# The last chunk of a three-product mixture layer, computed by Strassen on its two token halves

## The chip, the core and the metric

The kernel runs as one program on one core of a Trainium2 chip. The metric is the device time of one execution in microseconds (us). The kernel before took 1428.8, 1425.85 and 1426.25 us in three timed runs, median 1426.25.

## The reference

Three layers run one after the other: a linear attention with a norm, a dense gated mixture over 4608 tokens (512 wide, 1536 hidden), and a mixture of 8 experts of which each token takes one.

```python
x = attn_out.transpose(0, 2, 1, 3).reshape(4608, 512)
xn = x / sqrt(mean(x * x, -1) + 1e-6) * rms_g      # the first mixture
g, val = xn @ w_gate, xn @ w_val                   # 512 -> 1536
x = (silu(g) * val) @ w_out                        # 1536 -> 512
logits = x @ w_gate2                               # the second: 8 experts
e = argmax(logits)
out = prob[e] * (relu(x @ w1[e]) @ w2[e])          # 512 -> 1024 -> 512
```

The change is in `xn @ w_gate` and `xn @ w_val` for the last 512 tokens.

## The kernel before

**Tiling.** The 4608 tokens are 9 chunks of 512. Each fp32 product is three matmuls on split operands, high by high, low by high and high by low (`mm3`, L148); a `split` (L143) makes the high half on ScalarE (ACT) and the low half on VectorE (DVE). The hidden width is 12 tiles `f` of 128, each with a gate and a value half, so 24 `product`s a chunk. Chunks 0 to 3 take them plainly, 12 matmuls of 512 columns each. Chunks 4 to 7 go in two pairs by Strassen: seven products in the order 5, 1, 2, 6, 7, 3, 4 with weight sums that chunk 0 to 3 leave in DRAM (`wst`); class `Ring` (L1173) streams those on ACT's DMA queue into 3 slots of its own and 2 extra ones.

**Chunk 8 before** (L1958) is plain: for each `f` a gate product into the bank `pg`, SiLU on ACT (L1964), a value product into `pv`, and a multiplication on DVE (L1973). Class `Stream` (L1236) reads its weights back from `wst` on SyncE's (SP's) queue as tiles `lg` and `lv`, 512 KB each. The last `period` of chunks 6 and 7 (L1746) splits the chunk's inputs (`tstep`, L819 on ACT and L820 on DVE).

**What runs between the products.** After every product the code places pieces of other work by hand: `outs.drain(n)` gives n groups `po` of the down projection (an `mm3` of 512 columns; four groups take one 512 KB load of `wo` on SP's queue, L943, three buffers), `outs.stage` and `outs.low` split the hidden `h` into `ahl` (ACT L1651, DVE L1659), and `group()` (L1577) gives router logits of the chunk before (`junk`, DVE L992) and one step of the queue `rq`: `choose`, `exp`, `rank` and, after chunk 7, `order_step` and `start_expert`. `begin_route` (L1570) starts a chunk's route when its `po` groups are done and empties what is left of the route before.

**Towards the experts.** `rank` gives 28 small matmuls `rk` and ten small DVE operations, the last of which updates `acc`. `order_step` (L1335) counts tokens by a matmul `cnt` on `acc` and sorts the experts by load on DVE (L1346 to L1356) into `ordi`. SP reads `ordi` and loads expert weights `re` by it (L185), and `feed.step` (L292) splits them: `we` on ACT (L145), then its low half on DVE (L146). Each engine takes its instructions in the order in which they were issued.

Of the kernel before, what the change touches and what calls it, by code (L numbers as in the profile page):

```python
# [22 lines left out]
P = 128  # L23
# [22 lines left out]
AHL = 2  # L46
STAGED = 3
MORE = 2
LEFT = 7
SUPER = ((4, 5), (6, 7))  # L50
SINGLE = SUPER[0][0]
# [17 lines left out]
def attention_moe_kernel(  # L69
# [529 lines left out]
    def mark(kind, fn):  # L599
        kinds[fn] = kind  # L600
        return fn
# [571 lines left out]
    class Ring:  # L1173


        def __init__(self):
            ids = [(n, j) for _ in SUPER for n in range(2 * NPAIR) for j in range(7)]
            self.todo = deque(zip(ids[0::2], ids[1::2]))
            self.loaded, self.free, self.extra, self.done = deque(), RING, 0, []

        def fill(self, extra=MORE):
            while self.todo and (self.free or self.extra < extra):
                (n0, j0), (n1, j1) = self.todo[0]
                if n0 not in made or n1 not in made:
                    break
                own = self.free > 0
                if own:
                    self.free -= 1
                    w = rslot(f"r{n0}_{j0}")
                elif live[0] <= NSLOT - 3:  # L1190
                    self.extra += 1
                    w = wslot(f"r{n0}_{j0}")
                else:
                    break
                self.todo.popleft()
                d = w.bitcast(F32)
                if n0 == n1:
                    nc.scalar.dma_start(
                        d.rearrange("p (h n) -> p h n", h=2), blocks_of(n0, j0, j1)
                    )  # L1200
# [32 lines left out]
        if last and pn not in cur.apart:  # L1233
            live[0] -= 2

    class Stream:  # L1236


        def __init__(self):
            self.todo = deque((f, kind) for f in range(NF1) for kind in "gv")  # L1240
            self.free, self.held = RING, deque()

        def fill(self, tags=True):
            while self.todo and (self.free * tags or len(self.held) < 8 and live[0] <= NSLOT - 8):
                f, kind = self.todo.popleft()
                own = tags and self.free > 0
                w = (rslot if own else wslot)(f"l{kind}{f}")
                self.free -= own
                self.held.append(own)
                d, n = w.bitcast(F32), 2 * (f // 2) + (kind == "v")  # L1250
                if f % 2 == 0:
                    nc.sync.dma_start(d.rearrange("p (h n) -> p h n", h=2), blocks_of(n, 1, 2))
                else:
                    nc.sync.dma_start(d[:, 0:512], blocks_of(n, LEFT))
                    nc.sync.dma_start(d[:, 512:1024], blocks_of(n, 5))
                (wg if kind == "g" else wv)[f] = w

        def used(self):
            self.fill()
            own = self.held.popleft()  # L1260
            self.free += own
            live[0] -= not own

    class NextX:

# [284 lines left out]
    def start_feed():  # L1550
        feeds.append(feed)

    def flush_route():
        while logit_q:
            route.logit(*logit_q.popleft())
            if not logit_q:
                after_logits()
        while rq:
            rq.popleft()()

    def after_logits():
        r = route
        rq.extend([mark("v", r.choose), idle, idle, mark("t", r.exp), idle, mark("v", r.rank)])
        if r.c == 7:
            rq.extend([idle, idle, order_step])
            rq.extend(lambda i=i: start_expert(i) for i in range(3))
            rq.append(start_feed)
            rq.extend(lambda i=i: start_expert(i) for i in range(3, E))

    def begin_route(c, po):  # L1570
# [46 lines left out]
    gated, pace = set(), [0, 0]  # L1617

    class Out:

# [125 lines left out]
    def period(s, p, cur, nx):  # L1746
# [31 lines left out]
        def after(k):  # L1778
            if last and k == 0:
                while aux:  # L1780
                    aux.popleft()()
            barred = last and k == 4
            outs.drain(plan[k], s)
            outs.low()
            outs.stage()
            if not outs.ready and not outs.cur:
                outs.low()
            if p == 0 and cur.left:
                cur.more()
            elif nx and p > 7 and k in (0, 1, 4, 6) and not aux:  # L1790
                nx.more(2 if last else 5)
            elif last and k in (0, 1, 2, 4):
                tstep(8, (0, 1, 2, 0, 3)[k])
            elif last:
                stream.fill(False)
# [36 lines left out]
        after(6)  # L1832

    hs = []
    stream = Stream()

    for c in range(SINGLE):
        end = c == SINGLE - 1
# [117 lines left out]
    stream.fill()  # L1956
    for f in range(NF1):
        pg = psg.tile([P, 512], F32, tag="g", name=f"pg{c}_{f}")  # L1958
        if f % 2 == 0:
            h8 = hslot(f"h8_{f}")  # L1960
        h = h8[0][:, f % 2]
        product(pg, f, "g")
        stream.used()
        nc.scalar.activation(h, pg, AF.Silu)  # L1964
        for n in (3, 3) if f < 4 else (2, 1):
            outs.drain(n)
            outs.low()
            outs.stage()
            group(2 + (f < 4))
        pv = psg.tile([P, 512], F32, tag="v", name=f"pv{c}_{f}")  # L1970
        product(pv, f, "v")
        stream.used()
        nc.vector.tensor_tensor(h, h, pv, op=ALU.mult)  # L1973
        outs.add(c, h, h8[1])
        for n in (4, 3, 3) if f < 4 else (1, 0, 0):
            outs.drain(n)
            outs.low()
            outs.stage()
            group(2)
    live[0] -= KD  # L1980
    turned = False
    while outs.sets:
        if outs.sets[0]["left"] == 1 and not outs.cur and not turned:
# [244 lines left out]
```

## Time and profile before

| | |
|---|---|
| timed runs, median | 1426.25 us (1425.85 to 1428.8) |
| profiled execution, its own time | 1428.12 us |
| its span | 1426.2 us |
| TensorE (PE) busy in the span | 1404.1 us, 98% |
| VectorE busy | 918.2 us, 64% |
| ScalarE busy | 596.1 us, 42% |
| mean granted TensorE clock | 0.996 |
| chunk 8, from its first product to the first expert's transposes | 826.70 to 967.25 us |

The page gives busy time for each engine; matmuls are pipelined, so a matmul's duration is longer than the distance from its start to the next one's, and costs below are taken from starts. A bracket at the end of a timeline row is the engine's idle time ahead of it and what ended that.

### The profile page before, as it was taken

The page shows a single profiled execution, that of the slowest core. Times are in us where ns is not written, and L with a number is a line of the kernel's source. Part 1 is how long each engine was busy: PE and PEld are TensorE (multiplying, and loading weights), DVE is VectorE, ACT ScalarE, POOL GpSimd, SP SyncE. Part 2 cuts the span into 40 slices and gives each one's busy share as a digit, 9 for nine tenths or more (in the row PEclk, how much of TensorE's full clock was granted, in tenths as well). Part 3 has the DMA queues.
Part 4 walks back from the last instruction along what each step waited for, and adds up shares of the span by engine and source line. Part 5 has one row for each costly group of instructions (what it writes and reads, how often), then busy time and mean ns, then how long its engine had stood idle before and what let it go on. Part 6 is the DMA issues. An engine that isn't in the chain of part 4 may idle for free. (4 is left out here: it accounts for less than half of the span.)

```text
span 1426.2 us, 21177 instructions
## 1 busy us (share of the span) xinstructions
PE 1404.1 (98%) x7708; PEld 1182.4 (83%) x7708; DVE 918.2 (64%) x1931; ACT 596.1 (42%) x1112; POOL 200.1 (14%) x207
## 2 busy tenths in 40 slices
PE   7999999999999999999999999999999999999998
PEld 6777888878888878887888887889999989988986
DVE  5887775786778465565666356853553688578672
ACT  5775323333435433443232322243333556656651
POOL 2110101100220201001000100022404202302111
PEclk9999999999999999999999999999999999999999
DMA  7977735755763766567566575772423334334320
GB/s 239 304 231 253 249 116 175 261 184 190 235 218 111 264 231 212 175 208 257 197 204 195 163 265 193 221 237 75 144 75 122 104 109 144 121 106 141 121 82 35
DMA packets 112970, 255.52 MB, mean 179 GB/s; under 512 B 13803, under 2 KB 26347, under 8 KB 112864
## 3 DMA queue, kind: packets, MB, share of 16 engines
q1 hardware_dynamic: 81376, 190.24, 40.6%
q10 hardware_dynamic: 23040, 44.05, 9.7%
q0 software_dynamic: 8448, 19.85, 4.3%
q8 instruction: 62, 1.02, 0.3%
q14 instruction: 44, 0.36, 0.1%
HBM read 199.69 MB, written 55.28 MB: 179 GB/s over the span
## 5 line engine op out<-in xcount | busy, mean ns | idle before, releaser
L992 DVE SCALAR_TENSOR_TENSOR junk<-x,wgb 128x512 bf16<-128x512 f32 x256 | 189.4, 740 | 5.1 <-ACT x L968 0.2
L149 PE MATMUL po<-wo,ahl 128*128 128x512 f32 x408 | 160.6, 394 | 0.9 <-DVE x L970 0.9
L150 PE MATMUL po<-wo,ahl 128*128 128x512 f32 x408 | 159.0, 390 | 0.0
L151 PE MATMUL po<-wo,ahl 128*128 128x512 f32 x408 | 158.9, 390 | 0.0
L1227 PE MATMUL A<-xp,r 128*128 128x512 f32 x504 | 130.0, 393 | 1.0 <-DVE X L1812 0.8
L1065 POOL DMA_INDIRECT idxd<-rec,si x36 | 38.7, 1075 | 548.7 <-DVE cs L1074 447.1
L1227 PEld LDWEIGHTS A<-xp,r 128*128 128x128 f32 x504 | 93.3, 188 | 21.6 <-DVE X L1812 1.7
L1227 PE MATMUL X<-xp,r 128*128 128x512 f32 x360 | 93.4, 395 | 2.8 <-DMA r<-wst 1.2
L709 POOL TENSOR_TENSOR sg<-sq,smalls 128x512 f32<-128x512 f32 x36 | 49.5, 1377 | 319.5 <-ACT sq L691 242.1
L149 PEld LDWEIGHTS po<-wo,ahl 128*128 128x128 f32 x408 | 76.7, 188 | 17.1 <-DVE x L970 1.4
L151 PEld LDWEIGHTS po<-wo,ahl 128*128 128x128 f32 x408 | 76.6, 188 | 16.3
L150 PEld LDWEIGHTS po<-wo,ahl 128*128 128x128 f32 x408 | 76.6, 188 | 15.5
L1227 PEld LDWEIGHTS X<-xp,r 128*128 128x128 f32 x360 | 66.3, 188 | 18.4 <-ACT X L1803 2.0
L149 PE MATMUL pg<-x,wg 128*128 128x512 f32 x192 | 77.2, 402 | 0.1
L149 PE MATMUL pv<-x,wv 128*128 128x512 f32 x192 | 76.1, 397 | 0.6 <-DVE sl L1873 0.6
L151 PE MATMUL pg<-x,wg 128*128 128x512 f32 x192 | 75.1, 391 | 0.6 <-DVE x L820 0.6
L150 PE MATMUL pg<-x,wg 128*128 128x512 f32 x192 | 74.9, 390 | 0.6 <-DVE wg L928 0.6
L150 PE MATMUL pv<-x,wv 128*128 128x512 f32 x192 | 75.0, 391 | 0.0
L151 PE MATMUL pv<-x,wv 128*128 128x512 f32 x192 | 74.9, 390 | 0.0
L1874 ACT ACTIVATE ahl<-sl 128x512 fp32r<-128x512 f32 x42 | 26.5, 632 | 111.3 <-DVE sl L1873 111.3
L235 ACT ACTIVATE wo<-re 128x512 fp32r<-128x512 f32 x84 | 51.1, 626 | 31.8 <-DVE re L246 31.2
L1856 ACT ACTIVATE sl<-pg 128x512 f32<-128x512 f32 x48 | 28.7, 598 | 83.2 <-PE pg L151 68.1
(803 smaller groups left out, 3322.5 us busy)
## 6 DMA issues: line engine op xcount, KB each, us to landing
wo<-wos SPq DMA_DIRECT2D x90, 512.0 KB
r<-wst ACTq DMA_DIRECT2D x72, 512.0 KB
re<-in_moe_w SPq DMA_DIRECT2D x64, 512.0 KB
x1d<-x SPq DMA_DIRECT2D x32, 256.0 KB
k<-in_k SPq DMA_DIRECT2D x30, 256.0 KB
v<-in_v SPq DMA_DIRECT2D x30, 256.0 KB
q<-in_q SPq DMA_DIRECT2D x30, 256.0 KB
rg<-in_moe_w_gate SPq DMA_DIRECT2D x12, 512.0 KB
```

Source lines behind the costliest of these rows:

```text
L149: nc.tensor.matmul(ps, lhi, rhi, start=first, stop=False)
L150: nc.tensor.matmul(ps, llo, rhi, start=False, stop=False)
L151: nc.tensor.matmul(ps, lhi, rlo, start=False, stop=last)
L235: nc.scalar.activation(w[:, 0], part(n), AF.Copy)
L709: nc.gpsimd.tensor_tensor(sg, sq3, g2b[:, None, :].to_broadcast([P, 8, HD]), op=ALU.mult)
L992: nc.vector.scalar_tensor_tensor(j, self.rows[t], 1.0, wgb[e], op0=ALU.mult, op1=ALU.mult, accum_out=self.L[:, t, e : e + 1],)
L1065: nc.gpsimd.indirect_dma_start(out=idxd[:], out_offset=bass.IndirectOffsetOnAxis(ap=si[:, j : j + 1], axis=0), in_=rec[:, j, :], in_offset ...
L1227: nc.tensor.matmul(ps, w[:, a, kk, :], x[kk][b], start=first and kk == j == 0, stop=kk == 1 and j == 2, skip_group_check=True,)
L1856: nc.scalar.activation(sl, pg, AF.Silu)
L1874: nc.scalar.activation(ahl[:, 0:512], sl, AF.Copy)
```

## The change

Chunk 8's 24 plain products become 6 pairs of `f` by 7 Strassen products by gate and value: 84 products of six matmuls of 256 columns (L2020 of the new kernel). The two halves that Strassen needs are the chunk's two sets of 256 tokens, two halves of the contraction, and two neighbouring `f`. Each pair has accumulators `X` and `A` for the gate half, and `X..v` and `A..v` for the value half, the last two in banks of the pool that `rk` and `cnt` use too. Their results are put together between the products: copies on ACT after products 5 and 1 (L2036, L2038), additions on DVE after 6 and 7 (L2042, L2044), SiLU on ACT (L2031) and multiplications on DVE (L2033) for the four quarters of `h`. Because these banks are taken, `rank` and `order_step` are held (`hold`, `banked`) until a pair's last product is in; what is held of chunk 6's and 7's routes runs at the end of pairs 1 and 3.

`LastX` takes the place of the input splits: it turns the inputs, makes four sums, and splits seven operands, in the last period and in pair 0. `Stream` is gone; `Ring` has 42 more entries, each of two 256 KB loads, on SP's queue, with up to 6 extra slots. `PLAN` spreads 98 `po` groups over the pairs, 14 places in each. `feed.step` keeps more free slots while the ring has work.

```diff
+EXTRA = 6
+PLAN = (44,20,8,8,9,9)
...
             self.todo = deque(zip(ids[0::2], ids[1::2]))
+            self.todo.extend(
+                ((2 * i, j), (2 * i + 1, j)) for i in range(NPAIR) for j in range(7)
+            )
...
+                eng = nc.sync if len(self.todo) <= 7 * NPAIR else nc.scalar
...
-                    nc.scalar.dma_start(d[:, 0:512], blocks_of(n0, j0))
-                    nc.scalar.dma_start(d[:, 512:1024], blocks_of(n1, j1))
+                    eng.dma_start(d[:, 0:512], blocks_of(n0, j0))
+                    eng.dma_start(d[:, 512:1024], blocks_of(n1, j1))
...
-    class Stream:
+    class LastX:
...
+            if pn == "sum":
+                u = wslot("xu").bitcast(F32).rearrange("p (s k n) -> p s k n", s=2, k=2)
+                self.u = [u[:, i] for i in range(2)]
+                tt(self.u[0], b[0], b[1], op=ALU.add)
+                tt(self.u[1], self.u[0], a[0], op=ALU.subtract)
+                tt(b[0], b[0], a[0], op=ALU.subtract)
+                return
...
+            split(w[:, 0], w[:, 1], src)
...
+        banked.update((r.rank, order_step))
...
-        flush_route()
-        route = Route(c, po)
-        route.store()
+        flush_logits()
+        new = Route(c, po)
+        new.store()
+        if not hold[0]:
+            flush_route()
+        route = new
...
+            if hold[0] and fn in banked:
+                return True
...
-            feed.step(spare=2)
+            feed.step(spare=2 + (EXTRA - ring.extra) * bool(ring.todo))
...
-        product(pg, f, "g")
...
+    def between(k, g, i):
+        at, n = 2 * k + g, PLAN[i]
+        hold[0] = at < 13
+
+        def free(last):
+            while at == 13 and rq and (rq[0] is idle or rq[0] in banked):
+                if rq[0] is order_step and not last:
+                    break
+                rq.popleft()()
+
+        free(False)
+        ring.fill(EXTRA)
+        outs.drain((at + 1) * n // 14 - at * n // 14)
+        outs.low()
+        outs.stage()
+        lastx.more()
+        free(True)
+        group(2 if i < 2 else 1)
+
+    for i in range(NPAIR):
+        X = [psg.tile([P, 512], F32, tag="v", name=f"X8_{i}"), ptile(f"X8_{i}v")]
+        A = [psg.tile([P, 512], F32, tag="g", name=f"A8_{i}"), ptile(f"A8_{i}v")]
...
+        for k, pn in enumerate(ORDER):
+            for g in range(2):
...
+                        nc.tensor.matmul(
+                            ps, w[:, wq, kk, :], lastx.ops[pn][:, xq, kk],
+                            start=k < 2 and kk == j == 0, stop=kk == 1 and j == 2,
...
+                if pn == 5:
+                    nc.scalar.copy(s_, x)
+                elif pn == 1:
+                    nc.scalar.copy(x, a)
+                elif pn == 2:
+                    put(0, 0, x)
+                elif pn == 6:
+                    nc.vector.tensor_tensor(x, a, s_, op=ALU.add)
+                elif pn == 7:
+                    nc.vector.tensor_tensor(s_, a, s_, op=ALU.add)
+                    put(1, 1, s_)
...
+                between(k, g, i)
```

**Place 1, TensorE around the count of tokens.** `X` and `A` are accumulators, `xp` an operand of the inputs, `r` weight sums. Before:

```order
L149 MATMUL po_3_7950<-wo,ahl_8109 128x512
L150 MATMUL po_3_7950<-wo,ahl_8109 128x512
L151 MATMUL po_3_7950<-wo,ahl_8109 128x512
L1338 LDWEIGHTS ones
L1338 MATMUL cnt<-acc,ones 128x8
L149 MATMUL po_0_7947<-wo,ahl_8180 128x512
L150 MATMUL po_0_7947<-wo,ahl_8180 128x512
L151 MATMUL po_0_7947<-wo,ahl_8180 128x512
L149 MATMUL pv_8_8390<-x_0_7297,lv_8067 128x512
```

After:

```order
L151 MATMUL po_0_8024<-wo,ahl_8307 128x512
...
L1358 LDWEIGHTS ones
L1358 MATMUL cnt<-acc,ones 128x8
L2020 MATMUL X_4_8616<-xp_5_7365,r_0_8284 128x256 x6
L2020 MATMUL X_4v<-xp_5_7365,r_0_8284 128x256 x6
...
L2020 MATMUL A_4_8618<-xp_1_7387,r_1_8324 128x256 x6
L2020 MATMUL A_4v<-xp_1_7387,r_1_8324 128x256 x6
...
L2020 MATMUL X_4_8616<-xp_2_7390,r_2_8349 128x256 x6
L151 MATMUL po_3_8027<-wo,ahl_8307 128x512
...
L2020 MATMUL X_4v<-xp_2_7390,r_2_8349 128x256 x6
```

The count stood behind a gate product and two `po` groups after `rk`; now one `po` group is between. Behind it there were a `po` group and a 512-column product; now the products of pair 4, the third of which (product 2, `xp_2`) adds to what a copy on ACT leaves in `X_4` and `X_4v`. Each `po` group is three matmuls, of which one or two are shown; one more stands after `X_4v<-xp_5` and one after `A_4v<-xp_1`.

**Place 2, ScalarE where the first expert's weights are split.** `re_0`, `re_1` are raw expert weights. Before:

```order
L1964 ACT_TABLE_LOAD
L1964 ACTIVATE h_8_8295<-pg_8_8294 128x512
L1651 ACTIVATE ahl_8407<-h_8_8295 128x512
L145 ACTIVATE we_0_0_8446<-re_0_8358 128x512
L1964 ACTIVATE h_8_8295<-pg_9_8449 128x512
L145 ACTIVATE we_0_1_8489<-re_0_8358 128x512
L145 ACTIVATE we_1_0_8515<-re_1_8360 128x512
```

After:

```order
L2036 COPY s_4_8620<-X_4_8616 128x256
L2036 COPY s_4_8620<-X_4v 128x256
L2038 COPY X_4_8616<-A_4_8618 128x256
L147 ACTIVATE we_0_0_8689<-re_0_8584 128x512
L2038 COPY X_4v<-A_4v 128x256
L147 ACTIVATE we_0_1_8720<-re_0_8584 128x512
L2031 ACT_TABLE_LOAD
L2031 ACTIVATE h_4_8621<-X_4_8616 128x256
L147 ACTIVATE we_1_0_8758<-re_1_8586 128x512
```

The first split stood between a split of `h` and a SiLU; now it stands between the two copies L2038 that product 2 of pair 4 needs.

**Place 3, VectorE, the low halves of the same weights.** Before:

```order
L1973 TENSOR_TENSOR h_8_8295<-h_8_8295,pv_8_8390 128x512
L1659 TENSOR_TENSOR ahl_8407<-h_8_8295,ahl_8407 128x512
L146 TENSOR_TENSOR we_0_0_8446<-re_0_8358,we_0_0_8446 128x512
L146 TENSOR_TENSOR we_0_1_8489<-re_0_8358,we_0_1_8489 128x512
L146 TENSOR_TENSOR we_1_0_8515<-re_1_8360,we_1_0_8515 128x512
L1973 TENSOR_TENSOR h_8_8295<-h_8_8295,pv_9_8518 128x512
L146 TENSOR_TENSOR we_1_1_8555<-re_1_8360,we_1_1_8555 128x512
```

After:

```order
L1688 TENSOR_TENSOR ahl_8547<-h_3_8316,ahl_8547 128x512
L148 TENSOR_TENSOR we_0_0_8689<-re_0_8584,we_0_0_8689 128x512
L148 TENSOR_TENSOR we_0_1_8720<-re_0_8584,we_0_1_8720 128x512
L148 TENSOR_TENSOR we_1_0_8758<-re_1_8586,we_1_0_8758 128x512
L2033 TENSOR_TENSOR h_4_8621<-h_4_8621,X_4v 128x256
L148 TENSOR_TENSOR we_1_1_8786<-re_1_8586,we_1_1_8786 128x512
L2042 TENSOR_TENSOR X_4_8616<-A_4_8618,s_4_8620 128x256
```

The low half of `we_1_1` stood behind a multiplication and ahead of a low half of `h`; now it stands ahead of the addition of pair 4 that empties `A_4` after product 6.

**Place 4, SyncE's queue where chunk 8's weights begin.** Before:

```order
L943 DMA wo<-wos 128x1024 x9
L1254 DMA lg_7373<-wst_70 128x512
L1255 DMA lg_7373<-wst_70 128x512
...
L1252 DMA lg_7412<-wst_74 128x2x512
L1252 DMA lv_7414<-wst_75 128x2x512
L943 DMA wo<-wos 128x1024 x3
```

After:

```order
L945 DMA wo<-wos 128x1024
L1208 DMA r_1_7358<-wst_70 128x512
L1209 DMA r_1_7358<-wst_71 128x512
...
L1208 DMA r_1_7428<-wst_72 128x512
L1209 DMA r_1_7428<-wst_73 128x512
L945 DMA wo<-wos 128x1024 x2
L1208 DMA r_2_7477<-wst_72 128x512
```

Rows in the middle are left out. Before, twelve loads of the `Stream` lay between one `wo` load and the next; now it is fourteen of the `Ring`, and they stand after pair 0's own first load instead of inside the last period.

## Rows read from the trace of the kernel before

**Rows 1.** The page: span and TensorE's busy time.
```profile
span 1426.2 us, 21177 instructions
...
PE 1404.1 (98%) x7708; PEld 1182.4 (83%) x7708; DVE 918.2 (64%) x1931; ACT 596.1 (42%) x1112; POOL 200.1 (14%) x207
```

**Rows 2.** What TensorE waited for: line, releaser, total, times, longest (us).
```profile
PE po L149 <- DVE x L970: 0.9, 1, 0.9
```

**Rows 3.** Stretch of chunk 8: PE, PEld, DVE, ACT, POOL, clock, DMA, GB/s.
```profile
826.70:967.25 140.55, 139.61 (x644) 114.98 (x644) 89.91 (x235) 40.21 (x66) 16.32 (x16) 1.00 0.70 224
```

**Rows 4.** Timeline of TensorE, chunk 8's first product: start, duration (us).
```profile
826.76 0.39 PE L149 MATMUL pg<-x,lg 128*128 128x512 f32 x1
...
829.48 0.39 PE L149 MATMUL po<-wo,ahl 128*128 128x512 f32 x1
```

**Rows 5.** Timeline of TensorE, six-matmul products of 256 columns in an expert.
```profile
1376.46 0.88 PE L547 MATMUL X7a<-xs,wo 128*128 128x256 f32 x6
...
1379.33 0.93 PE L547 MATMUL X7a<-xs,wo 128*128 128x256 f32 x6
...
1386.88 0.88 PE L547 MATMUL X7a<-xs,wo 128*128 128x256 f32 x6
```

**Rows 6.** Timeline of TensorE from the first `rk` to the count `cnt`.
```profile
926.37 0.18 PE L1047 MATMUL rk<-ohb,tri 128*128 128x8 bf16 x1
...
926.73 0.47 PE L149 MATMUL pg<-x,lg 128*128 128x512 f32 x1
...
930.90 0.18 PE L1338 MATMUL cnt<-acc,ones 128*128 128x8 bf16 x1
```

**Rows 7.** Timeline of VectorE: a multiplication, first and last operations of `rank`.
```profile
925.95 0.69 DVE L1973 TENSOR_TENSOR h<-h,pv 128x512 f32<-128x512 f32 x1 [3.81 <-PE pv L151]
926.91 0.19 DVE L1052 TENSOR_TENSOR rk<-rk,baser 128x32 f32<-128x32 f32 x1 [0.27 <-PE rk L1050]
...
928.46 0.17 DVE L1075 TENSOR_TENSOR acc<-acc,cs 128x8 bf16<-128x8 bf16 x1
```

**Rows 8.** Timeline of SyncE's queue where the first experts' weights are loaded.
```profile
935.04 2.85 SPq L185 DMA_DIRECT2D re<-in_moe_w  x3
```

**Rows 9.** Timeline of ScalarE and VectorE splitting those weights.
```profile
939.13 0.63 ACT L145 ACTIVATE we<-re 128x512 fp32r<-128x512 f32 x1 [3.08 <-DMA re<-in_moe_w]
939.67 0.58 ACT L1964 ACTIVATE h<-pg 128x512 f32<-128x512 f32 x1
...
943.17 0.63 ACT L145 ACTIVATE we<-re 128x512 fp32r<-128x512 f32 x1 [2.40 <-DMA re<-in_moe_w]
...
943.83 0.69 DVE L146 TENSOR_TENSOR we<-re,we 128x512 fp32r<-128x512 f32 x1 [2.34 <-ACT we L145]
944.44 0.68 DVE L1973 TENSOR_TENSOR h<-h,pv 128x512 f32<-128x512 f32 x1
```

**Rows 10.** Costs of 256-column operations, ScalarE's and VectorE's groups by line.
```profile
L554 ACT COPY X7a<-A7a 128x256 f32<-128x256 f32 x2 | 0.7, 357 | 0.7 <-PE A7a L547 0.3 <-ACT sums L552 0.3
...
L558 DVE TENSOR_TENSOR X7a<-A7a,sums 128x256 f32<-128x256 f32 x2 | 0.9, 433 | 1.4 <-PE A7a L547 1.4
```

**Rows 11.** SyncE's queue, first and last of twelve loads for chunk 8.
```profile
821.43 0.38 SPq L1254 DMA_DIRECT2D lg<-wst  x1
...
827.77 0.37 SPq L1252 DMA_DIRECT2D lv<-wst  x1
```

**Rows 12.** Busy time by stretch (columns as in group 3) while those loads ran.
```profile
820.00:830.00 10.00, 10.00 (x48) 8.26 (x47) 4.90 (x8) 2.16 (x4) 0.00 (x0) 1.00 0.79 278
830.00:840.00 10.00, 10.00 (x46) 8.29 (x45) 3.48 (x6) 3.25 (x6) 0.00 (x0) 1.00 0.79 300
```

**Rows 13.** The same view near the program's start.
```profile
4.00:8.00 4.00, 1.28 (x18) 0.82 (x17) 0.00 (x0) 0.00 (x0) 0.13 (x1) 1.00 1.02 250
8.00:12.00 4.00, 3.11 (x31) 2.77 (x32) 0.58 (x3) 0.34 (x2) 0.00 (x0) 0.56 1.06 362
12.00:16.00 4.00, 4.00 (x45) 3.67 (x45) 1.45 (x3) 2.15 (x4) 2.42 (x2) 0.59 1.03 397
```

More of the change, by code (lines that the diff above doesn't have):

```diff
@@ L1189, in fill @@
                     w = rslot(f"r{n0}_{j0}")
-                elif live[0] <= NSLOT - 3:
+                elif live[0] <= NSLOT - (3 if extra == MORE else 6):
                     self.extra += 1
@@ L1197, in fill @@
                 if n0 == n1:
-                    nc.scalar.dma_start(
+                    eng.dma_start(
                         d.rearrange("p (h n) -> p h n", h=2), blocks_of(n0, j0, j1)
@@ L1234, in part, with turn, more @@
             live[0] -= 2
-    class Stream:
+    class LastX:
         def __init__(self):
[L1240 to L1262, printed above, removed]
+            self.ops, self.t, self.left = {}, [], deque(("sum", *ORDER[:3], "sum3", *ORDER[3:]))
+        def turn(self, kk):
+            if kk % 2 == 0:
+                w = wslot(f"xt{kk}").bitcast(F32)
+                self.t.append(w.rearrange("p (k n) -> p k n", k=2))
+            ps = ptile(f"xT8_{kk}")
+            for j in range(4):
+                nc.tensor.transpose(ps[:, j * P : j * P + P], xo[:, j, kk * P : kk * P + P], ident)
+            nc.scalar.activation(
+                self.t[kk // 2][:, kk % 2], ps, AF.Copy, scale=comb[:, kk : kk + 1]
+            )
+        def more(self):
+            if not self.left:
+                return
+            pn = self.left.popleft()
+            a, b = ([t[:, :, o : o + HALF] for t in self.t] for o in (0, HALF))
+            tt = nc.vector.tensor_tensor
+            if pn == "sum":
[4 more added lines that the diff above has]
+                tt(b[0], b[0], a[0], op=ALU.subtract)
+                return
+            if pn == "sum3":
+                tt(self.u[0], a[1], self.u[1], op=ALU.subtract)
+                return
+            src = {
+                5: self.u[0], 6: self.u[1], 7: b[0], 3: self.u[0], 1: a[0], 2: a[1], 4: b[1],
+            }[pn]
+            w = wslot(f"xp8_{pn}").rearrange("p (s k n) -> p s k n", s=2, k=2)
+            split(w[:, 0], w[:, 1], src)
+            self.ops[pn] = w
+            if not self.left:
+                live[0] -= 3
@@ L1551, in start_feed, with flush_logits @@
         feeds.append(feed)
-    def flush_route():
+    def flush_logits():
         while logit_q:
@@ L1557, in flush_route @@
                 after_logits()
+    def flush_route():
+        flush_logits()
         while rq:
@@ L1571, in begin_route @@
         nonlocal route
-        flush_route()
-        route = Route(c, po)
-        route.store()
+        flush_logits()
+        new = Route(c, po)
[3 more added lines that the diff above has]
+        route = new
         logit_q.extend((t, e) for t in range(4) for e in range(8))
@@ L1614, in group @@
         if feeds and sum(w is not None for w in experts[0].w1 + experts[0].w2) < 2 * NF2:
-            feed.step(spare=2)
-    gated, pace = set(), [0, 0]
+            feed.step(spare=2 + (EXTRA - ring.extra) * bool(ring.todo))
+    gated, pace, banked, hold = set(), [0, 0], set(), [False]
     class Out:
@@ L1791, in after @@
                 nx.more(2 if last else 5)
[L1792 to L1795, printed above, removed]
+            elif last and not nx and k in (0, 1, 2, 4):
+                lastx.turn((0, 1, 2, 0, 3)[k])
+            elif last and not nx and k > 4:
+                lastx.more()
+                lastx.more()
             n = ((1, 1, 0, 0, 1, 0, 2), (2, 1, 1, 0, 2, 1, 2))[s][k]
@@ L1834, in attention_moe_kernel @@
     hs = []
-    stream = Stream()
+    lastx = LastX()
     for c in range(SINGLE):
@@ L1955, in attention_moe_kernel @@
     outs.open(c)
[L1956 to L1961, printed above, removed]
-        product(pg, f, "g")
[L1963 to L1979, printed above, removed]
@@ L1980, in attention_moe_kernel @@
-    live[0] -= KD
+    while not {5, 1, 2} <= set(lastx.ops):
+        lastx.more()
+    def between(k, g, i):
[11 more added lines that the diff above has]
+        outs.stage()
+        lastx.more()
+        free(True)
+        group(2 if i < 2 else 1)
@@ new lines, in attention_moe_kernel, with put @@
+    for i in range(NPAIR):
+        X = [psg.tile([P, 512], F32, tag="v", name=f"X8_{i}"), ptile(f"X8_{i}v")]
+        A = [psg.tile([P, 512], F32, tag="g", name=f"A8_{i}"), ptile(f"A8_{i}v")]
+        s5 = ap1.tile([P, 512], F32, tag="sl", name=f"s58_{i}").rearrange("p (g n) -> p g n", g=2)
+        h8, used = hslot(f"h8_{i}")
+        for k, pn in enumerate(ORDER):
+            for g in range(2):
+                x, a, s_ = X[g][:, :HALF], A[g][:, :HALF], s5[:, g]
+                ps = x if pn in (5, 2, 3) else a
+                w, end = ring.take(2 * i + g, k)
+                for kk in range(2):
+                    for j, (wq, xq) in enumerate(((0, 0), (1, 0), (0, 1))):
+                        nc.tensor.matmul(
+                            ps, w[:, wq, kk, :], lastx.ops[pn][:, xq, kk],
+                            start=k < 2 and kk == j == 0, stop=kk == 1 and j == 2,
+                            skip_group_check=True,
+                        )
+                if end is not None:
+                    ring.done.append(end)
+                def put(r, f, src):
+                    dst = h8[:, f, r * HALF : r * HALF + HALF]
+                    if g == 0:
+                        nc.scalar.activation(dst, src, AF.Silu)
+                    else:
+                        nc.vector.tensor_tensor(dst, dst, src, op=ALU.mult)
+                if pn == 5:
[9 more added lines that the diff above has]
+                    put(1, 1, s_)
+                elif pn == 3:
+                    put(0, 1, x)
+                else:
+                    put(1, 0, a)
+                if i == NPAIR - 1 and g == 1:
+                    live[0] -= 1
+                if (k, g) == (6, 1):
+                    for j in range(2):
+                        outs.add(c, h8[:, j], used)
+                between(k, g, i)
```

## The prediction

> **What bounds the kernel now.** I read the page's busy times first: TensorE (PE) is busy for 1404.1 of 1426.2 us [rows 1]. The view of what PE waited for comes next; within chunk 8 it has one entry, 0.9 us for the copies that `begin_route` makes [rows 2]. The stretch of chunk 8 says the same: 139.61 of 140.55 us busy, at the full clock, with VectorE at 64% and the DMA engines moving 224 GB/s [rows 3]. So PE is the bound, what a change takes off PE here shows in full, and so does every wait that it adds. The reader should see how little slack that leaves: what stands behind PE today is covered by PE's own long runs of 512-column work.
>
> **The matmuls.** From the first `pg` matmul to the first `po` behind it are 829.48 − 826.76 = 2.72 us [rows 4], one product of twelve matmuls, 0.227 us each. 24 of them are 65.3 us. The new products are six matmuls of 256 columns. The trace has this form in an expert: four of them took 1379.33 − 1376.46 = 2.87 us, 0.7175 each, 0.120 a matmul; fourteen, with evacuations in between that PE waits a little for, took 10.42, 0.744 each [rows 5]. 84 of them are 60.3 us, or 62.5. I take 60.3, since in chunk 8 `po` groups (3 × 0.227 = 0.68 us each) lie between most of the products: **−5.0**, at the worst −2.8. The `po` groups are the same work as before.
>
> The Trainium skill, page "TensorE: Matmul & The Clock Gate", section "Back-to-back issue gap", speaks against the change: in a sustained stream of weight loads and matmuls it gives 81 ns for 128 columns and 131 ns for 512, so that halving the columns is far from halving the time. An estimate on the line between its two figures is 98 ns for 256, three quarters of the 512 figure, and the sum by it would be 504 × 98 − 288 × 131, a loss of 11.7 us. The trace does not agree: 0.227 and 0.120 us are a ratio of 0.53 [rows 4, 5].
>
> **The wait of `begin_route`** [rows 2] goes. A product of pair 1 now stands between that `po` group and the copies it waits for: **−0.9**.
>
> **The operands.** Four input splits become four turned copies and seven splits on ACT, and four sums and seven low halves on DVE. That is some eleven DVE operations of 0.69 [rows 7] for four, about 4.8 us more, in a stretch where DVE is busy for 4.9 of 10 us and ACT for 2.2 [rows 12]; that is the cover. At the border to pair 0 they lie close. Call t the start of pair 0's first matmul: the third needs the low half of operand 5, at t + 0.24. DVE has a multiplication, three sums and that low half to do in a row, behind a product that ends one product half and two `po` groups before t, 2.72 us by the 0.227 pace. It starts 0.27 after that (as worked out for `cnt` below), and five operations at 0.61 (943.83 to 944.44) [rows 9] and the last one's 0.08 more end at t + 0.7: **+0.4** (0 to 0.8). One more operation ahead of these would make it 1.1.
>
> **`wo` behind the ring.** Where the last period issued twelve loads of 4.2 MB in 821.43 to 827.77 [rows 11] well ahead, SP now issues fourteen of 256 KB, 3.67 MB, around pair 0's start and only then the next `wo` (Place 4). SP takes about 0.53 us for each, 7.4 us in all. The burst begins when a `wo` buffer came free two `po` groups earlier, about t − 1.0. PE needs the `wo` behind it after ten `po` groups and five products, t + 6.8 + 3.6 = t + 10.4. Burst and load are 4.19 MB. At 289 GB/s, the mean of the two stretches where the old burst ran [rows 12], they land after 14.5 us, t + 13.5, 3.1 late; at 397 GB/s, the highest rate of a stretch [rows 13], at t + 9.6, in time. I take **+2.0** (0 to 3.1), nearer to the rows of the same loads.
>
> **VectorE in the pairs.** A pair has eight 256-column operations of 0.433 [rows 10] for two multiplications of 0.69 [rows 7], 2.1 us more on 23. At 64% [rows 3] that fits, but in pairs 2 and 3 a logit follows each product and DVE is nearly full: **+0.3** (0 to 1).
>
> **The count.** `cnt` needs `acc`, the end of `rank`. Before, `rk` took 926.37 to 926.73 and `cnt` came at 930.90, 4.2 us after it [rows 6], behind a product and two `po` groups, while `acc` was ready at 928.63 [rows 7]. Now one `po` group (0.68) is between (Place 1). Let e be the end of pair 3's last product on PE's schedule. The multiplication starts 0.27 after it (925.95, against 926.37 less one `po` group) [rows 6, 7], takes 0.43, and `rank` 1.72 (926.91 to 928.63) [rows 7]: `acc` is there at e + 2.42. PE reaches `cnt` at e + 0.36 + 0.68. It waits **+1.4** (1.0 to 2.1, if a logit gets in between). Behind `cnt` on PE is all of pair 4, so nothing hides it.
>
> **The expert weights.** This is the term that decides. `re_0` depends on `cnt`: issue at 935.04, first use on ACT at 939.13 after an idle 3.08 us [rows 8, 9], so it is usable 8.2 us after `cnt` (call it c) [rows 6]; `re_1` at 943.17, c + 12.3. Nothing shortens this chain. Before, ACT waited there too, but only a SiLU and a split of `h` stood behind it, and PE had work. Now ACT's copy of `A_4v` into `X_4v` is queued behind the first split (Place 2), and product 2 of pair 4 on the value half cannot start before it. PE reaches that product after five products and three groups, c + 3.6 + 2.0 = c + 5.65. The copy is done at c + 8.2 + 0.54 (the split's pace, 939.13 to 939.67) + 0.36 [rows 9, 10], c + 9.15: **+3.5**. Bounds: the issue is 4.1 after c at any rate, and 512 KB at 397 GB/s [rows 13] take 1.3, so the load can't be usable before c + 5.4, a wait of 0.7; ring loads in the same queue could delay it, and I allow 6.
>
> Product 7 of pair 4 needs `A_4` emptied, by an addition on DVE that is queued behind the low half of `we_1_1` (Place 3), so behind `re_1`. DVE starts `we_1_0`'s low half at c + 12.9 (943.83) [rows 9]; that, one multiplication, one more low half and the addition take 0.61 + 0.43 + 0.61 + 0.43, to c + 15.0. PE, already late, gets there at 9.15 + three products + two groups = c + 12.7: **+2.3** (0 to 5). After that DVE's queue alternates splits and additions, and I count 0.3, 0.6 and 0.3 at the two value products of 7 and 4 and at pair 5's first: **+1.2** (0 to 3).
>
> **Sum.** −5.0 − 0.9 + 0.4 + 2.0 + 0.3 + 1.4 + 3.5 + 2.3 + 1.2 = **+5.2 us**. The profiled execution took 1428.12 us with a span of 1426.2, so the changed one by this sum 1433.3. The profiled execution is 1.9 above the median of the runs, 1426.25; on that median the forecast is **1431.4 us**.
>
> **Rivals.**
> *Faster: the weights come in time.* From `re_0` at c + 4.8 or earlier (below the bound above) nothing is left of 3.5; from `re_1` at c + 10 nothing of 2.3. More likely both come partly sooner, since chunk 8's weights are loaded up to nine ahead and DMA is at 224 GB/s, and DVE's lag vanishes. With the `wo` term hidden, −5.0 − 0.9 + 0.4 + 1.4 + 0.3 + 0.7 is −3.1, **1423.2 us**. For it: the matmul gain is the surest number. Against it: ACT's idle 3.08 and 2.40 us [rows 9] stand in the same chain. Chance 0.25.
> *No change.* `re_1` lands with `re_0` and the `wo` is in time: 5.2 − 2.3 − 2.0 = +0.9, **1427.2 us**. Chance 0.20.
> *Slower by the clock.* Near the start PE was busy for 1.28 of 4 us, and in the next two stretches it ran at 0.56 and 0.59 of the clock [rows 13], the 1.2 GHz level for most of 7 us. Waits of 3.5 and 2.3 us within 6 us of work come near that. At half speed for 7 us PE loses about 3.4 us: **1434.8 us**. Chance 0.07. The Trainium skill, page "TensorE: Matmul & The Clock Gate", section "HAM oscillation — how this bites in real kernels", tells of TensorE falling back to its low clock where it waits for DMA between short bursts; by that rule this would happen, and the rows near the start agree.
> *Slower by the DMA.* Pair 4 must bring pair 5's ring loads, `wo` and expert weights at once. If `re_0` and `re_1` land 2 us later each, 3.5 and 2.3 grow by 2 together, and the terms behind by as much: **1435.5 us**. It decides from a rate above some 300 GB/s in this stretch. Chance 0.10.
> *The change doesn't do what it says.* If a fixed part made a 256-column matmul cost three quarters of a 512-column one, 504 × 0.170 − 65.3 would be a loss of 20 us, 25 worse than above, **1456 us**; the 0.120 [rows 5] speaks against it: chance 0.01. Three quarters is the proportion that the section on the issue gap, quoted above from the Trainium skill, comes to.
>
> **How the numbers follow.** The forecast itself, 1429.2 to 1434, has 0.37. About 0.2% (2.85 us) is what a measurement of this kernel can tell from no change. Slower: 0.37 + 0.07 + 0.10 + 0.01 = 0.55; same 0.20; faster 0.25. The range has to take in most of the faster case and the DMA case: 1422 to 1436.5, with about 0.1 left out on each side. The forecast's own range is 1429.2 to 1434.
>
> **What would show it.** Right: in the profile after, products of six at 0.72 us; a wait of PE at the first `X..v` of product 2 for ACT's copy L2038 of 3 to 4 us, one for DVE L2042 of about 2, one of `cnt` for DVE of about 1.4, one of a `po` group for `wo` early in chunk 8. Wrong: chunk 8's stretch shorter than before with PE waits under 3 us in all; or a granted clock below 1.00 in pair 4; or PE waiting for the ring's weights, which no term has.

## The result, and the profile after

The changed kernel took 1438.27 us (median of five runs, 1435.39 to 1446.12) against 1426.62 before: a ratio of 1.0078 with a 95% interval of 1.0062 to 1.0095. That is 11.65 us slower where 5.2 were forecast, so the sign was right and the size was not, and the time lies above the forecast range of 1422 to 1436.5. Two slow runs with times far above the rest, one of `again` (1552.71 us) and one of the kernel before (3625.38 us), are left out of every median below.

The page of the profiled execution after, as [rows 1] (span, then busy times):

```profile
span 1433.4 us, 21856 instructions
PE 1403.6 (98%) x7920; PEld 1190.6 (83%) x7920; DVE 930.4 (65%) x1973; ACT 610.1 (43%) x1154; POOL 199.5 (14%) x207
```

The span is 7.2 us longer, and TensorE's (PE's) busy time is nearly the same: what was added is idle time. What PE waited for from 826 us to the border of the experts, as [rows 2] (line, releaser, total, times, longest):

```profile
PE X_4v L2020 <- ACT X_4v L2038: 2.4, 1, 2.4
PE po L151 <- DMA wo<-wos: 1.9, 1, 1.9
PE cnt L1358 <- DVE acc L1077: 1.1, 1, 1.1
PE A_4v L2020 <- DVE s L2044: 0.8, 1, 0.8
PE X L2020 <- DVE xp L148: 0.3, 1, 0.3
PE po L152 <- DVE ahl L1688: 0.2, 1, 0.2
PE X_5v L2020 <- DVE h L2033: 0.2, 1, 0.2
```

The same view of the time ahead of chunk 8; the kernel before has none of these three:

```profile
PE A L1233 <- ACT xp L147: 1.3, 1, 1.3
PE po L151 <- DMA wo<-wos: 1.2, 1, 1.2
PE A L1233 <- DMA r<-wst: 1.0, 1, 1.0
```

Two stretches of busy time, with the columns of [rows 3]: chunk 8 from its first product to the first expert's first product, and 8 us inside it.

```profile
828.39:974.11 145.72, 138.78 (x861) 122.82 (x859) 104.76 (x281) 53.54 (x109) 15.95 (x16) 0.99 0.85 289
936.00:944.00 8.00, 7.51 (x42) 7.04 (x43) 5.21 (x10) 5.16 (x10) 0.97 (x1) 0.79 1.00 350
```

Chunk 8 took 145.72 us; from its first product at 826.76 to the first `h0a` matmul at 967.29 it was 140.53 before. That is +5.2. In the second row PE's granted clock is 0.79: for a part of those 8 us it stood at the 1.2 GHz level.

The first Strassen product of the first chunk pair starts at 474.36 before and at 473.12 after, and the first expert's first product at 967.29 and 974.11. In PE's timelines, before and then after:

```profile
474.36 1.62 PE L1227 MATMUL X<-xp,r 128*128 128x512 f32 x6 [1.20 <-DMA r<-wst]
...
967.29 0.28 PE L149 MATMUL h0a<-xh0a,we 128*128 128x256 f32 x1
```

```profile
473.12 1.66 PE L1233 MATMUL X<-xp,r 128*128 128x512 f32 x6
...
974.11 0.28 PE L151 MATMUL h0a<-xh0a,we 128*128 128x256 f32 x1
```

From the first of these products to chunk 8 it was 352.4 us, and is 355.3. So the profiled execution has +2.9 us ahead of chunk 8, +5.2 in it, and 0.9 less in all the rest. The two stretches serve as a measure in the table of all kernels below; they are taken from starts in the timeline of PE.

### The profile page after: what moved, and what is told of

The parts are those of the page before. It is cut to its first block, busy times and chain, and to the rows that moved or that the text cites. A ratio compares the mean times of both kernels' runs of the same rounds, so it can differ in the third digit from the quotient of the medians.

```text
span 1433.4 us, 21856 instructions
## 1 busy us (share of the span) xinstructions
PE 1403.6 (98%) x7920; PEld 1190.6 (83%) x7920; DVE 930.4 (65%) x1973; ACT 610.1 (43%) x1154; POOL 199.5 (14%) x207
## 3 DMA queue, kind: packets, MB, share of 16 engines
q8 instruction: 64, 1.05, 0.3%
```

## The experiments

| kernel | median us | ratio to before, 95% | to chunk 8 | chunk 8 |
|---|---|---|---|---|
| before | 1426.6 to 1427.6 | | 352.4 | 140.5 |
| after | 1438.27 | 1.0078 (1.0062 to 1.0095) | 355.3 | 145.7 |
| again | 1438.68 | 1.0085 (1.0069 to 1.0100) | 355.4 | 145.3 |
| late | 1440.27 | 1.0094 (1.0079 to 1.0110) | 356.1 | 148.1 |
| late_wo | 1439.33 | 1.0088 (1.0072 to 1.0103) | 354.5 | 146.6 |
| late_wo_cnt | 1439.72 | 1.0092 (1.0078 to 1.0106) | 354.8 | 146.7 |
| ring3 | 1433.94 | 1.0053 (1.0039 to 1.0066) | 351.0 | 145.8 |
| before_ring6 | 1431.74 | 1.0035 (1.0022 to 1.0048) | 355.4 | 141.9 |
| ring3_calm | 1429.69 | 1.0017 (1.0008 to 1.0025) | 351.4 | 143.5 |
| ring3_calm_wo | 1429.90 | 1.0018 (1.0009 to 1.0027) | 351.5 | 141.3 |
| tail | 1429.26 | 1.0011 (1.0002 to 1.0019) | 351.7 | 140.9 |
| tail_cnt | 1429.43 | 1.0014 (1.0006 to 1.0023) | 351.6 | 140.0 |
| full | 1427.62 | 1.0005 (0.9996 to 1.0014) | 352.3 | 139.3 |

"To chunk 8" is from the first Strassen product to chunk 8's first, and "chunk 8" from there to the first expert's first product, both in us of the profiled execution of each kernel. Each ratio is to runs of the kernel before that were timed along with that kernel; the medians of the kernel before differ by 1 us between them.

**again: the changed kernel once more.**

> The changed kernel as it is, for a second profile and more times. In the first profile chunk 8 (its first product to the first expert's first product) took 145.7 us against 140.5 before, +5.2, which is what was forecast, while the median of the runs is 11.6 us above that of before. Theory A (the clock): the waits of TensorE in pair 4 and the wait for wo in pair 0 drop it to the 1.2 GHz level, for 3.4 us in the first profile and for longer in other executions, so times scatter between 1435 and 1446 us with the mean granted clock, and a profile of a slower execution shows a low clock inside 828 to 975 us. Theory B (elsewhere): the scatter is at the start of the program, as in the profile of before (0.56 at 8 to 16 us), and chunk 8 costs +5 us in every execution; then a slower profile shows chunk 8 at 145 to 146 us again.

Measured: 1438.68 us. The stretches are 355.4 and 145.3 us, and the seven waits of chunk 8 are there, with one more of 1.0 us for the addition in front of product 7:

```profile
PE A L2020 <- DVE X L2042: 1.0, 1, 1.0
```

But the clock is different, in the same places:

```profile
928.00:936.00 8.00, 6.06 (x41) 5.19 (x39) 4.06 (x20) 1.73 (x5) 2.42 (x2) 1.00 0.40 139
936.00:944.00 8.00, 5.69 (x37) 4.93 (x38) 5.21 (x10) 5.27 (x10) 0.97 (x1) 1.00 1.01 351
```

Here it is 1.00 all the way, with PE idle at the same places as in the execution above. So the clock's fall in pair 4 is something that some executions have and others don't; it costs up to 1.7 us where it comes (8 us at 0.79), and chunk 8 is 4.8 us longer than before without it too. Theory A as the main cause of chunk 8's time falls; whether the clock makes the scatter of the other runs is taken up at the end of the next section. Theory B, that the rest is at the start of the program, doesn't fit either: what is constant beside chunk 8's +5 are the 3 us between 474 and 828 us.

**late, late_wo, late_wo_cnt: hold the expert splits, pace the ring, cover the count.** Each has the edits of the one before. `quiet` stops the splits, and the second argument of `ring.fill` is the most loads that one call may issue:

```diff
-        if feeds and sum(w is not None
+        if not quiet[0] and feeds and sum(w is not None
...
         hold[0] = at < 13
+        quiet[0] = i == 4 and at < 9
...
-        ring.fill(EXTRA)
+        ring.fill(EXTRA, (2 if at == 0 else 1) if i == 0 else 99)
...
         lastx.more()
+        if i == 3 and at == 13:
+            outs.drain(2)
         free(True)
```

> The splits of the expert weights are held until product 7 of pair 4 (ninth of its fourteen products); the loads start as before. Theory A: the waits for ACT's copy L2038 (2.4 us), for DVE L2044 (0.8) and L2033 (0.2) go, the clock stays at 1.00 in pair 4, and the median falls by 4 (waits alone) to 9 us (waits and clock): 1429 to 1434. Theory B: it falls by about 4 and the scatter stays. A third reading, that the loads rather than the order of the queues hold PE up (DMA near its limit in pairs 4 and 5): the wait moves to pair 5 and the median falls by less than 2.

> As late, and in pair 0 the ring's loads are issued two at the first place and one at each later one, so that wo is no longer behind fourteen loads. All theories: the wait of po for wo at 841 us (1.9 us) goes; 2 us below late. If PE then waits for the ring's weights in pair 0 instead, the gain is under 1.

> As late_wo, and two more po groups at the end of pair 3 between rk and cnt. The wait of cnt (1.1 us) goes; 1 us below late_wo. With all three waits gone and no clock loss, by theory A what is left is the matmuls' gain of 5.0 and the 0.9 of begin_route, less 0.4 for the operands and about 1 us for the changes between 256- and 512-column work: 1426.6 - 4.5, some 1422 us, faster than the kernel before. By theory B it stays above 1426.

Measured: 1440.27, 1439.33 and 1439.72 us, no gain at all. The largest of what PE waited for in chunk 8 of `late`:

```profile
PE X L2021 <- ACT X L2039: 5.2, 1, 5.2
PE po L151 <- DMA wo<-wos: 1.7, 1, 1.7
PE cnt L1358 <- DVE acc L1077: 1.1, 1, 1.1
```

The waits of pair 4 are gone, and one of 5.2 us has come in pair 5. ACT's timeline in `late` and PE's show it (the bracket is the idle time ahead):

```profile
946.95 0.36 ACT L2037 COPY s<-X_5v 128x256 f32<-128x256 f32 x1
953.19 0.63 ACT L147 ACTIVATE we<-re 128x512 fp32r<-128x512 f32 x1 [5.88 <-DMA re<-in_moe_w]
953.72 0.36 ACT L2039 COPY X<-A 128x256 f32<-128x256 f32 x1
```

```profile
954.14 1.65 PE L2021 MATMUL X<-xp,r 128*128 128x256 f32 x6 [5.24 <-ACT X L2039]
```

It is the same fault one pair later. With the splits later, a raw buffer comes free later, the next loads start at 945.47, and the first lands only as ACT's 5.88 us of idle end. The copy that PE needs stands behind that split. Six 256-column matmuls then take 1.65 us instead of 0.88, at the lower clock, as the stretch after shows:

```profile
952.00:960.00 8.00, 5.86 (x23) 5.47 (x24) 4.13 (x7) 4.86 (x10) 1.77 (x3) 0.57 0.89 327
```

So the clock came down after the wait of 5.2 us here (0.57) and after the same wait in `late_wo` (4.6 us, 0.57), and by less in `late_wo_cnt` (4.9 us, 0.79). The third reading of the expectation is what happened, except that the queue's order is still half of it. The pacing took the wait for `wo` from 1.7 to 0.6 us. Two more groups ahead of `cnt` took that wait away and brought two for hidden tiles that were not split yet, 1.2 and 1.0 us: nothing won.

**ring3 and before_ring6: one comparison, put back in the one kernel and put into the other.** Behind the waits ahead of chunk 8 stands a line of the change that the excerpt of the diff ahead of the prediction leaves out. `Ring.fill` takes an extra slot only if enough are free, and the change asks for 6 instead of 3 wherever `extra` is not `MORE` (2). Chunk 8 calls it with 6; but `period` calls it with 1 from its period 9 on (9 to 11 in the first chunk pair, where `nx` is set):

```python
more = (MORE if p < 9 else 1) if 0 < p < 11 + (nx is not None) else 0
```

The edit of `ring3` on the changed kernel, and that of `before_ring6` on the kernel before:

```diff
-                elif live[0] <= NSLOT - (3 if extra == MORE else 6):
+                elif live[0] <= NSLOT - (3 if extra <= MORE else 6):
```

```diff
-                elif live[0] <= NSLOT - 3:
+                elif live[0] <= NSLOT - (3 if extra == MORE else 6):
```

> The changed kernel with one comparison of the ring put back: 3 free slots are asked for wherever at most MORE extra loads are allowed, 6 only in chunk 8. In the change, the periods 9 and 10 of the first chunk pair, which allow one extra load, came under the limit of 6 as well. Theory C (the change reaches back): in the five profiles of the changed kernel and its variants the time from the first Strassen product to chunk 8's first product was 354.5 to 356.1 us against 352.4 before, with waits of 1.3 us for a split (at 631 us) and 1.0 to 1.8 us for the ring's weights (at 661) that before does not have. Then these waits go, this stretch is 352 to 353 us, and the median falls by 2.5 to 3 us, to 1436 to 1437. Theory A or B as sole cause: no change beyond 1 us.

> The kernel before with that one limit alone: 6 free slots instead of 3 for the ring's extra load in periods 9 and 10. Theory C: 2 to 3 us slower than before, with the waits at 631 and 661 us. Otherwise: no difference.

Measured: `ring3` 1433.94 us, 4.3 below `after` and 4.7 below `again` by the medians, 3.6 and 4.6 by the ratios to before (1.0053 against 1.0078 and 1.0085); its interval lies below that of `again` and overlaps that of `after` by 0.0004. `before_ring6` took 1431.74 us, which is 4.1 us above before by the medians and 5.0 by the ratio, 1.0035 (1.0022 to 1.0048), clear of no effect. The stretch to chunk 8 moves with the line: 351.0 us in `ring3`, 355.4 in `before_ring6`. The timeline of PE around the place, of after and of `before_ring6`:

```profile
631.01 1.62 PE L1233 MATMUL A<-xp,r 128*128 128x512 f32 x6 [1.32 <-ACT xp L147]
...
661.29 0.71 PE L1233 MATMUL A<-xp_0q,r 128*128 128x512 f32 x2 [0.96 <-DMA r<-wst]
```

```profile
632.25 1.61 PE L1227 MATMUL A<-xp,r 128*128 128x512 f32 x6 [1.24 <-ACT xp L145]
```

`ring3` has neither wait. The order of ACT's queue suggests how: without the extra load (603.94 in `ring3`), its slot goes to splits of the next pair's operands (613.60 in `after`), and the ring's next load with two halves is issued at 621.64 instead of 616.89. ACT's timeline of `ring3`, then of `after`:

```profile
603.94 0.37 ACTq L1204 DMA_DIRECT2D r<-wst  x1
...
616.89 0.34 ACTq L1208 DMA_DIRECT2D r<-wst  x1
```

```profile
613.60 1.14 ACT L147 ACTIVATE xp<-xa 128x512 fp32r<-128x512 f32 x2
...
621.64 0.34 ACTq L1208 DMA_DIRECT2D r<-wst  x1
```

The wait of 1.3 us comes and goes with the line in both kernels. The one at 661 us for the ring's weights goes with it in the changed kernel, but is not in `before_ring6`, so the line alone doesn't make it. PE's starts, compared with `ring3` place by place, give the line 1.6 us at 631 and 1.2 us at 661 in `after`, 1.6 and 1.9 in `again`. The third wait ahead of chunk 8 in `after`, 1.2 us for `wo`, is not the line's: it stands at 478 us, ahead of period 9, and `again` doesn't have it.

In `before_ring6` only 1.5 of the 3.0 us ahead of chunk 8 stand at 632. Two loads of chunk 8's weights that the kernel before issues at 633 us are missing there, and PE idles ahead of chunk 8's first product, which comes 1.3 us later for it; chunk 8 is 1.3 us longer too. The changed kernel has no `Stream`, so this part of the 4 to 5 us can't be carried over to it:

```profile
830.40 0.47 PE L149 MATMUL pg<-x,lg 128*128 128x512 f32 x1 [1.18 <-DVE ahl L1659]
```

Theory C holds; its size in the changed kernel is what `ring3` gives back.

**ring3_calm, ring3_calm_wo: hold the splits until their loads have landed.** Both have the line of `ring3`, `quiet` in front of the splits as in `late`, and another condition for it:

```diff
         hold[0] = at < 13
+        quiet[0] = at < (9 if i == 4 else 7 if i == 5 else 0)
```

> As ring3, and the splits of the expert weights are held in pair 4 until its tenth product and in pair 5 until its eighth, when their loads have landed. (With the hold in pair 4 alone the wait came back in pair 5, 5.2 us for the copy into X behind the split of re_3.) If the queue order on ACT and DVE makes the wait, PE waits for no copy in pairs 4 and 5, the clock stays at 1.00 there, and the median falls by 3 to 7 us below ring3. If the loads themselves are late, a wait for the experts shows up at the first expert instead and less than 2 us are won.

> As ring3_calm, with pair 0's ring loads issued one by one. The wait for wo in pair 0 (1.5 to 1.9 us) falls to 0.6 or less: 1 to 1.5 us below ring3_calm. If all three causes are right, chunk 8 to the first expert takes 140.5 - 5.0 - 0.9 + 0.5 + 1.2 + 1.1 + 0.5 = 138 us, and the median is 1425 us or below, level with the kernel before or faster; if it stays above 1430, something else of the change costs more than these three.

Measured: `ring3_calm` 1429.69 us, 4.3 below `ring3`; no copy and no addition of pairs 4 and 5 is waited for any more. `ring3_calm_wo` took 1429.90 us: no difference that can be told, where 1425 or below was expected. Its chunk 8 is 2.2 us shorter in the profile, but not by the pacing: the wait for `wo` is 1.1 us there and 0.2 in `ring3_calm`. Up to 1.7 of the 2.2 are the clock, which fell in `ring3_calm` and not in `ring3_calm_wo`:

```profile
960.00:968.00 8.00, 8.00 (x36) 6.60 (x35) 4.25 (x8) 3.41 (x6) 2.47 (x3) 0.79 0.46 146
```

Of the waits of chunk 8 in `ring3_calm`, two are new:

```profile
PE po L152 <- DVE ahl L1688: 2.0, 1, 2.0
PE po L151 <- ACT h L2032: 1.4, 1, 1.4
```

The splits now crowd the end of pair 5, ahead of the last hidden tiles.

**tail, tail_cnt, full: keep them off the last hidden tiles too.** `tail` is `ring3_calm` with another hold in pair 5; `tail_cnt` adds one group ahead of `cnt`; `full` adds the pacing of `late_wo`.

```diff
-        quiet[0] = at < (9 if i == 4 else 7 if i == 5 else 0)
+        quiet[0] = at < 9 if i == 4 else not 6 <= at < 11 if i == 5 else False
...
+        if i == 3 and at == 13:
+            outs.drain(1)
...
         outs.group()
+        quiet[0] = bool(outs.half) or any(t["stage"] for t in outs.sets)
         group(2)
```

> As ring3_calm, with the hold in pair 5 from the twelfth product on until the last hidden tiles are split, because ring3_calm showed the expert splits ahead of those on ACT and DVE: PE waited 2.0 us for the last ahl and 1.4 us for the hidden tile before it. If these are the last of the moved waits, both go, the first product of chunk 8 to the first expert takes 140 us or less (143.5 in ring3_calm, 140.5 before), and the median falls by about 3 us, to 1426 to 1427, level with the kernel before. If the splits then hold up the expert itself, the time from there to the end grows from 452 us by as much and nothing is won.

> As tail, with one more po group between rk and cnt at the end of pair 3 (two more made PE wait for hidden tiles later). The wait of cnt falls from 1.1 to 0.4 us: 0.7 us below tail, some 1425 to 1426, not to be told from tail with certainty.

> All four mends together: the ring's limit of 3, the hold of the expert splits as in tail, one more po group ahead of cnt, and pair 0's ring loads one by one. By stages, chunk 8 to the first expert was 140.0 us in tail_cnt, of which 1.7 is the wait for wo in pair 0; without it 138.3 us, 2.2 below the kernel before, and the stretch from the first Strassen product to chunk 8 is 351.5, 0.9 below. If stages add up, the median is about 3 us below the kernel before, 1424 to 1425; if it stays at +2 us as tail did, the remainder lies outside these two stretches.

Measured: 1429.26, 1429.43 and 1427.62 us. Chunk 8 falls to 140.9, 140.0 and 139.3 us, about 1 us less far than expected, and the medians of `tail` and `tail_cnt` can't be told from that of `ring3_calm`. In `tail` the waits of 2.0 and 1.4 us are gone, but PE waits 2.2 us for `wo`. From the first expert's first product to the end it is 460.4 us in `tail`, 458.9 before (not the 452 of the expectation) and 459.3 to 460.9 in the other kernels, so no delay of the expert shows. What PE still waits for in chunk 8 of `full`:

```profile
PE po L151 <- DMA wo<-wos: 0.7, 1, 0.7
PE po L151 <- ACT ahl L1681: 0.5, 1, 0.5
PE cnt L1359 <- DVE acc L1077: 0.4, 1, 0.4
PE X L2024 <- DVE xp L148: 0.3, 1, 0.3
PE po L152 <- DVE ahl L1689: 0.2, 1, 0.2
```

`full` is level with the kernel before, 1.0005 (0.9996 to 1.0014); nothing here beats it. The expectation of 3 us below it was missed: chunk 8 is 1.2 us shorter than before, not 2.2, and the median is 0.8 above.

## Why the prediction was right or wrong

**The step that failed is the reach of the change.** The prediction let the change begin in the last period of chunks 6 and 7 ("the operands") and costed nothing before it. One comparison in `Ring.fill` acts from period 9 of the first pair on. In the profiled executions it costs 2.8 us in `after` and 3.5 in `again`, and putting it back takes 3.6 to 4.7 us off the timed runs, more than half of the 6.4 us that were missed. It had a line in the whole diff, and the prediction has no term for it: a term was put at nothing without a reason. No rival covered it. Two of the signs that the prediction named for being wrong came in `after`: PE waited for the ring's weights (1.0 us at 661 us), and the granted clock fell below 1.00 in pair 4. With the line put back, `ring3` is 7.6 us above before by its ratio (5.6 to 9.4), still somewhat more than the 5.2 of the sum.

**Matmuls: −5.0, right, less a term that was not there.** A product takes 0.71 us in the trace after. But eleven products and 42 matmuls of `po` (872.13 to 889.68) take 17.55 us, where 11 × 0.7175 + 42 × 0.2267 is 17.41. That is 0.013 us more per product, an estimate of 1.1 us for 84. It stands in the `po` matmuls, whose starts in chunk 8 are 0.232 us apart in the median, 0.227 before. That passing between the two sizes makes it is argued: no run changes the alternation alone. The Trainium skill, page "TensorE: Matmul & The Clock Gate", section "Back-to-back issue gap", has figures for 128 and 512 columns, by which the prediction's estimate was a loss; the trace doesn't agree: 0.12 us for 256 columns stands in chunk 8 as it stood in [rows 5].

**`begin_route`, the border, `wo`, `cnt`: right.** The forecast was −0.9, 0.4, 2.0 and 1.4; measured were: gone, 0.3, 1.9 and 1.1. The term of 0.3 for VectorE in pairs 2 and 3 was not there: PE waits for nothing between 842 and 927 us.

**The expert weights: mechanism right, the sizes partly.** Product 2 of pair 4 was to wait 3.5 us for ACT's copy behind the split of `re_0`, and waited 2.4, since `re_0` was usable 7.4 us after `cnt`, not 8.2, and PE came 0.35 us later than counted, as the timelines of PE and of ACT in `after` show:

```profile
928.14 0.17 PE L1358 MATMUL cnt<-acc,ones 128*128 128x8 bf16 x1 [1.05 <-DVE acc L1077]
...
936.49 1.65 PE L2020 MATMUL X_4v<-xp,r 128*128 128x256 f32 x6 [2.35 <-ACT X_4v L2038]
```

```profile
935.53 0.63 ACT L147 ACTIVATE we<-re 128x512 fp32r<-128x512 f32 x1 [3.77 <-DMA re<-in_moe_w]
936.07 0.37 ACT L2038 COPY X_4v<-A_4v 128x256 f32<-128x256 f32 x1
```

The 2.3 us at product 7 measured 1.0 in `again` and `ring3`, because `re_1` had landed with `re_0`: ACT waits for no load between the two. In `after` that wait is missing although the loads landed alike, because PE was at the lower clock and came later: from the second row of PE above to product 7 it is 4.95 us there and 4.78 in `again`, of which 0.99 is the wait. The 1.2 behind them measured 0.8 and 0.2. `late` shows that it is the order of the queue and the landing together: moved by itself, the wait comes back elsewhere, and larger.

**The clock, a rival with 0.07, came in part.** That second row has the six matmuls at 1.65 us, 0.79 of the clock over 8 us. The Trainium skill, same page, section "HAM oscillation — how this bites in real kernels", tells of TensorE falling to its low clock where it waits for DMA between short bursts; `late` agrees (5.2 us of wait, 0.57), and so does the first execution of the changed kernel; `again` and `ring3` have nearly the same waits and the clock at 1.00.

**The sum of chunk 8 came out exactly, +5.2, by luck.** The waits forecast come to 11.1 us and those measured to 6.9. The clock's 1.7 (part of it in place of the wait at product 7) and the 1.1 in the `po` matmuls took most of the place of the difference, and the rest is a little at each wait that the view of waits doesn't count: `cnt` starts 1.44 us after the `po` matmul ahead of it (926.70), at whose pace 0.23 is due, and the view has 1.05. That is 0.16 more, and six of the seven waits have it.

**What stays open.** The stages of the profiled executions add up to +7.2 us, the medians to +11.65. The profiled execution before (1428.12) is 1.5 us above its kernel's median, and the one after (1435.39) 2.9 below its own. In `after`, `ring3` and `ring3_calm_wo` the profiled execution is the shortest of its kernel's runs or close to it, and no profile shows a run of `after` of its median or above. `again`, 2.5 us longer than `after` in the profile, has 1.2 more ahead of 474 us and 1.6 more behind the first expert's first product, so outside the two stretches the same kernel varies by 2.8 us. `tail` is 2 us above before, with both stretches level; its profile has 0.8 and 1.5 us at the same two places.

The granted clock of each timed run is on record, and may be part of it. In `after` it falls as the time rises: 0.998 at 1435.39 us, 0.996 and twice 0.995 at the next three, 0.991 at 1446.12. The kernels that have the line of `Ring.fill` and the splits in the way (`after` to `late_wo_cnt`) have 0.994 to 0.995 in the mean of their runs, before and `ring3` 0.997. An estimate: 0.002 of 1430 us is some 3 us. It is not shown: the two longest runs of `ring3` have the highest clock of the five, 0.999.

## What to carry to other kernels

Where PE is 98% busy, a change that shortens its work is decided by the work that it had been hiding: list for each new short product what stands ahead of its evacuation on its engine, and what that waits for. An instruction that waits for a load must not stand in front of one that PE needs, and moving it needs the load's landing time, not a fixed number of places. And for a changed condition in a shared helper, look at every caller: here a comparison meant for one stage cost 3.6 to 4.7 us in another.

## What the runs showed of the hardware

In chunk 8 after, the 512-column matmuls between products of 256 columns start 0.232 us apart in the median, and 0.227 in chunk 8 before, where all have 512. A wait cost PE 0.16 us beyond the idle time that the view counts, in six of the seven waits of chunk 8 after. The granted clock fell after the waits of 4.6 to 5.2 us in all three kernels that had one (0.57, 0.57 and 0.79 over 8 us). Around waits of 1.9 to 2.4 us it fell in two executions out of five (0.79 in `after` and `ring3_calm`; not in `again`, `ring3` and `ring3_calm_wo`). The loads of expert weights took 3.5 to 8.4 us from issue to landing, median 6.4, in the changed kernel, where the DMA engines moved 350 to 385 GB/s around them, against 4.1 us from issue to first use for the first one before.
